# Twenty weight blocks narrowed behind group 0's last tile, and row tile 0's first products of mixture 1 with the weights stationary

## The chip, the cores and the metric

The kernel runs on one core of a Trainium2 chip. The metric is the time of one execution on the device, in microseconds; lower is better. The engines named here are TensorE (PE; PEld is its loading of stationary operands), VectorE (DVE), ScalarE (ACT), GpSimd (POOL) and SyncE (SP), which issues most transfers.

## The reference

Three stages follow one another. Attention over 2 batches of 8 heads, 576 positions and 64 channels keeps the 32 largest scores of each row. Its output, as 1152 tokens of 512 channels, goes through a dense layer pair with SiLU, and the result through eight experts, all of which see every token and are summed with weights from a Sinkhorn normalisation:

```python
scores = scale * np.matmul(q, k.transpose(0, 1, 3, 2))
kth = np.partition(scores, -top_k, axis=-1)[..., -top_k:-top_k + 1]
scores = np.where(scores >= kth, scores, -1000000000.0)
attn = np.exp(scores - np.max(scores, axis=-1, keepdims=True))
attn = attn / (np.sum(attn, axis=-1, keepdims=True) + 1e-09)
x = attn @ v                                   # 1152 x 512
h = x @ w_in                                   # 512 -> 2048
x1 = (h * (1.0 / (1.0 + np.exp(-h)))) @ w_out  # 2048 -> 512
for e in range(E):                             # 8 experts, 512 -> 1024 -> 512
    out += P[:, e:e + 1] * (np.maximum(x1 @ w1[e], 0.0) @ w2[e])
```

The weights w_in and w_out come as 8-byte values; the rest is 4-byte.

## The kernel before

The 1152 tokens are nine row tiles of 128, in five groups: tile 0 alone is group 0, tiles 1 and 2 are group 1, and so on in pairs. For each group, attention goes over four pairs of heads. One score tile (`score_tile`) is 128 rows of one head: TensorE makes the scores (L310), ScalarE copies them (L313), VectorE finds the 32 largest by four MAX8 (L322) with three MATCH_REPLACE between them (L328), ScalarE takes the exponential (L326), VectorE masks and sums (L331) and takes the reciprocal (L334), ScalarE normalises (L335), TensorE transposes in five pieces (L338, L340), ScalarE copies these out (L351, L352), and TensorE multiplies by v (`pav`, L348). For tile 0 the result is x0; for later groups it is split into a high and a low part, xH and xL. The tiles of q are turned by TensorE in a PSUM pool with the tag "pp" and come out as qq and qL.

Mixture 1 (w_in, SiLU, w_out) and the experts follow. For tile 0 mixture 1 is a function of its own, `first_row`, since its weights arrive then. They are 32 blocks of 128 x 512 values, 0.5 MB each; 0 to 15 are w_in (block 4c + F is rows c and columns F), 16 to 31 are w_out. Each is loaded into one of four raw buffers (RAWB, L500) and narrowed to 4 bytes by `narrow`: ScalarE takes the high words (L467), GpSimd (L473), or for each third block ScalarE (L471), the low words into one of CVN buffers cv_n, and VectorE puts the two together (L476). For blocks from LATE on, this last step is issued only behind `held`, the last reciprocal of group 0; the tiles of group 1 wait for the same instruction to be issued. A narrowed copy of each block is written to HBM (L507, `kept_in` and `kept_out`), from which mixture 1 of the later groups reads; all 32 writes are issued behind the last load.

In `first_row` the hides (L518) have x0 as the stationary operand and 512 weight columns moving; F = 0, 1, 2 gather in three PSUM banks, and F = 3 in the bank that F = 0 leaves. A silu is a tanh by ScalarE (L525) and a product by VectorE (L526, gr_m). Its result has tokens on the partitions, so TensorE transposes it (L531) and ScalarE copies it out (L535) before the second products (L540). `x1_tile` then copies x1 (L665), transposes it (L668) and splits it into x1H and x1L, the input of the experts.

Behind that, the kernel fills TensorE's time with expert work on the tiles that are done (FILL): experts 0 to 5 on tile 0, then mixture 1 of group 1, experts 6 and 7 on tile 0, mixture 1 of group 2, and so on. Expert weights come through SP's queue into `raw` (L608) and are split by ScalarE (L135) and GpSimd (L136) into `wa`. The three PSUM banks pass from `first_row` to the experts and the mixtures in this order.

What runs when is decided as the program is built: a scheduler orders each engine's instructions by priorities (`tc.cur_priority`; `conv_at` for narrowings, `keep_at` for the writes), by data and buffers, and by `tc.issue_after`, which keeps an instruction behind another in that ordering. Each engine then runs its own list in order.

## Time and profile before

| | us |
|---|---|
| median of 3 runs | 1257.95 |
| the runs, lowest to highest | 1255.61 to 1258.76 |
| the profiled execution | 1257.62 |
| its span | 1255.8 |
| TensorE busy | 1191.3 (95%) |
| VectorE busy | 811.9 (65%) |
| ScalarE busy | 595.1 (47%) |
| GpSimd busy | 562.9 (45%) |

The page adds up the busy time of each engine over the span. The stretches and timelines further down give the same for parts of it, from the start of the span. A record of the timeline may stand for several instructions of one kind (x4); then its time is from the first one's start to the last one's end. Records of neighbouring instructions overlap, since an instruction starts before the one ahead of it has written its last value. A bracket at the end of a record is idle time ahead of it and what ended that.

### The profile page before, as it was taken

Reading aid. Unit: us, or ns where it says so; the run is one execution under the profiler, and the core shown is the slowest. Engines: PE = TensorE matmul, PEld = TensorE weight load, DVE = VectorE, ACT = ScalarE, POOL = GpSimd, SP = SyncE. Lnnn points to the kernel's source line nnn. Section 1 sums busy time; section 2 is a strip of 40 time slices with the busy share of each in tenths; the row PEclk is TensorE's granted clock in tenths of the full one; section 3 lists DMA queues with packets and bytes.
Section 4 is the critical chain, followed back from the end, with each engine's and each line's share of the span. In section 5 each row is a group of like instructions: output and inputs, shape, how many; then the busy total and the mean of one; then the engine's idle time right before and its main releaser. Section 6 shows DMA issues by size and latency. Waiting matters only on the chain.

```text
span 1255.8 us, 17731 instructions
## 1 busy us (share of the span) xinstructions
PE 1191.3 (95%) x6030; PEld 942.5 (75%) x6030; DVE 811.9 (65%) x1567; ACT 595.1 (47%) x1173; POOL 562.9 (45%) x633
## 2 busy tenths in 40 slices
PE   5868999999999899999998999999999999999998
PEld 3544666688767778889686888888888888888886
DVE  7999999999999999113556434545434445344443
ACT  6855878887866676323313242223322323323221
POOL 6731766678712462320735444344443443353310
PEclk9889999999999999999998999999999999999999
DMA  8994776998776789999724121131121211211002
GB/s 268 296 361 146 231 244 204 323 355 306 240 262 218 241 289 319 325 350 371 264 84 141 53 66 45 41 84 34 52 66 34 75 43 34 68 51 46 23 1 67
DMA packets 131722, 210.90 MB, mean 168 GB/s; under 512 B 23472, under 2 KB 69552, under 8 KB 131632
## 3 DMA queue, kind: packets, MB, share of 16 engines
q1 hardware_dynamic: 131632, 209.77, 50.0%
q8 instruction: 48, 0.79, 0.3%
q14 instruction: 42, 0.34, 0.1%
HBM read 170.15 MB, written 39.58 MB: 167 GB/s over the span
## 4 chain that ended last, share of the span: by engine, by line
PE 75%; DVE 19%; ACT 2%; issue 1%; DMA 1%; POOL 1%; SPq 0%; DVEq 0%; ACTq 0%; POOLq 0%
PE h L145 8%; PE h L146 8%; PE h L144 8%; DVE m L322 6%; DVE w L328 5%; PE bank L144 4%; PE bank L146 4%; PE bank L145 4%; PE yA L146 4%; PE yA L145 4%; PE yA L144 4%; PE yB L144 4%; PE yB L145 4%; PE yB L146 4%; PE bank L582 4%; DVE s L331 2%
## 5 line engine op out<-in xcount | busy, mean ns | idle before, releaser
L136 POOL TENSOR_TENSOR wp<-rw,wp 128x512 fp32r<-128x512 f32 (+1 forms) x56 | 86.2, 1559 | 207.3 <-ACT wp L135 207.3
L322 DVE MAX8 m<-w 128x8 f32<-128x576 f32 x192 | 141.3, 752 | 0.8
L136 POOL TENSOR_TENSOR wa<-raw,wa 128x512 fp32r<-128x512 f32 x88 | 114.8, 1318 | 39.3 <-ACT wa L135 26.9
L136 POOL TENSOR_TENSOR w<-rw,w 128x512 fp32r<-128x512 f32 x56 | 73.0, 1306 | 98.6 <-ACT w L135 98.6
L328 DVE MATCH_REPLACE8 w<-m,w 128x576 f32<-128x576 f32 x128 | 95.2, 746 | 0.0
L144 PE MATMUL yB<-w,gH_0b 128*128 128x512 f32 x208 | 80.9, 389 | 0.0
L145 PE MATMUL yB<-w,gH_0b 128*128 128x512 f32 x208 | 80.9, 389 | 0.0
L951 DVE SCALAR_TENSOR_TENSOR gL_0b<-gB,gH_0b 128x512 fp32r<-128x512 f32 (+1 forms) x56 | 45.2, 808 | 55.1 <-ACT gH_0b L950 54.3
L146 PE MATMUL yB<-w,gL_0b 128*128 128x512 f32 x208 | 80.1, 389 | 0.0
L950 ACT ACTIVATE gH_0b<-gB 128x512 fp32r<-128x512 f32 (+1 forms) x56 | 33.6, 600 | 76.5 <-PE yB L145 43.5
L146 PE MATMUL h<-x1H,wp 128*128 128x512 f32 x168 | 66.9, 398 | 0.0
L144 PE MATMUL h<-x1H,wp 128*128 128x512 f32 x168 | 66.9, 398 | 0.0
L145 PE MATMUL h<-x1L,wp 128*128 128x512 f32 x168 | 66.7, 397 | 0.0
L136 POOL TENSOR_TENSOR gL_m<-g_m,gH_m 128x256 fp32r<-128x256 f32 x48 | 37.6, 783 | 59.7 <-ACT gH_m L135 59.5
L964 DVE TENSOR_TENSOR gB<-u,h 128x512 f32<-128x512 f32 x56 | 38.5, 687 | 37.4 <-PE h L146 37.3
L144 PE MATMUL bank<-xH,wa 128*128 128x256 f32 x192 | 57.1, 297 | 5.9 <-DVE g_m L433 5.7
L135 ACT ACTIVATE w<-rw 128x512 fp32r<-128x512 f32 x56 | 34.7, 627 | 57.4 <-PE yB L146 48.3
L331 DVE SCALAR_TENSOR_TENSOR s<-s,m,e 128x576 f32<-128x576 f32 x64 | 61.7, 963 | 0.3
L326 ACT ACTIVATE e<-s,sm 128x576 f32<-128x576 f32 x64 | 49.9, 781 | 21.8 <-DVE s L331 15.4
L582 PE MATMUL bank<-wb,gT_e 128*128 128x512 f32 x128 | 58.4, 595 | 0.4 <-ACT gT_e L601 0.4
L335 ACT ACTIVATE s<-s,sm 128x576 f32<-128x576 f32 x64 | 50.1, 784 | 16.6 <-DVE sm L334 16.2
L135 ACT ACTIVATE wa<-raw 128x512 fp32r<-128x512 f32 x88 | 54.7, 645 | 1.6 <-DMA raw<-kept_in 0.9
(366 smaller groups left out, 3631.2 us busy)
## 6 DMA issues: line engine op xcount, KB each, us to landing
wa<-sk SPq DMA_DIRECT2D x64, 512.0 KB, 5.4
wb<-sk SPq DMA_DIRECT2D x64, 512.0 KB, 5.1
rw<-in_moe_w_dram SPq DMA_DIRECT2D x112, 256.0 KB, 2.8
raw<-in_moe_w_dram SPq DMA_DIRECT2D x80, 256.0 KB, 3.6
wb<-in_moe_w_dram SPq DMA_DIRECT2D x32, 512.0 KB, 4.6
sk<-wa SPq DMA_DIRECT2D x24, 512.0 KB, 4.0
sk<-wb SPq DMA_DIRECT2D x24, 512.0 KB, 4.5
wfr<-in_moe_w_in_dram SPq DMA_DIRECT2D x16, 512.0 KB, 5.6
```

The source lines that it names most:

```text
L135: nc.scalar.activation(dH, src, AF.Copy)
L136: eng.tensor_sub(dL, src, dH.bitcast(F32))
L144: nc.tensor.matmul(ps, wH, xH, start=first, stop=False, skip_group_check=more)
L145: nc.tensor.matmul(ps, wH, xL, start=False, stop=False, skip_group_check=more)
L146: nc.tensor.matmul(ps, wL, xH, start=False, stop=last, skip_group_check=more)
L322: nc.vector.max(mr, src)
L326: nc.scalar.activation(e, s, AF.Exp, scale=SCALE, bias=sm[:, 0:1])
L328: nc.vector.match_replace(out=w, in_to_replace=mr, in_values=src, imm_value=-3e38)
L331: nc.vector.scalar_tensor_tensor(s, s, m8[:, TOPK - 1 : TOPK], e, op0=ALU.is_ge, op1=ALU.mult, accum_out=sm[:, 1:2])
L335: nc.scalar.activation(s, s, AF.Copy, scale=sm[:, 3:4])
L582: nc.tensor.matmul(y, gT[:, c * P : (c + 1) * P], b[c], start=F == 0 and c == 0, stop=F == nF - 1 and c == NDC - 1)
L951: nc.vector.scalar_tensor_tensor(gL, src, 0.0, gH.bitcast(F32), op0=ALU.max, op1=ALU.subtract)
```

## The change

In `narrow`, LATE falls from 26 to 12, so VectorE's step of 20 blocks, not 6, is issued behind group 0's last reciprocal. CVN grows from 4 to 5, and four more buffers for low words, for blocks 12 to 15, are cut out of the tiles (`cv_xH`, `cv_xL`) that group 1's x uses later. The writes of the first 12 narrowed blocks are issued behind load 24, the other 20 behind the last load.

In `first_row` a weight block of 128 x 128 is now the stationary operand and the 128 rows of x0 move: 64 products in place of 16, and the result has the hidden channels on the partitions. The transposes and their copies (`turned`) are gone. F = 3 has a PSUM bank of its own, taken from the pool "pp" in which q is turned. The silu is written over its own tanh (`g_m0`), and the second products gather in bank 1. `held` becomes the silu of F = 2 once `first_row` is written, so group 1's tiles are issued behind that. `opened`, the copy x1H of tile 0, holds back the normalisations of group 1's first head pair and some of its exponentials. The hides of c = 2, apart from F = 0, come behind the last transposes of group 0.

```diff
-CVN = 4
-LATE = 26
+CVN = 5
+LATE = 12
...
     def evac_split(dH, dL, ps):
-        nc.scalar.activation(dH, ps, AF.Copy)
+        ins = nc.scalar.activation(dH, ps, AF.Copy)
         nc.vector.tensor_sub(dL, ps, dH.bitcast(F32))
+        return ins
...
-                nc.scalar.activation(e, s, AF.Exp, scale=SCALE, bias=sm[:, 0:1])
+                with tc.issue_after(behind.ins) if behind and late else nullcontext():
+                    nc.scalar.activation(e, s, AF.Exp, scale=SCALE, bias=sm[:, 0:1])
...
-        nc.scalar.activation(s, s, AF.Copy, scale=sm[:, 3:4])
+        with tc.issue_after(behind.ins) if behind else nullcontext():
+            nc.scalar.activation(s, s, AF.Copy, scale=sm[:, 3:4])
...
-        nc.tensor.transpose(pt2, s[:, S - P : S], ident)
+        heads.append(nc.tensor.transpose(pt2, s[:, S - P : S], ident))
...
+                                     opened if (g, p) == (1, 0) else None, i == 1)
...
+    spare = []
...
-        n = cvp.tile([P, W], I32, name=f"cv_n_{i}", tag="cvn", bufs=CVN)
+        n = spare.pop(0) if i >= LATE and spare else cvp.tile([P, W], I32, name=f"cv_n_{i}", tag="cvn", bufs=CVN)
...
+        for i in "HL":
+            t = xps[0].tile([P, NDC, 256], F32R, name=f"cv_x{i}", tag=f"x{i}").bitcast(I32).rearrange("p c t -> p (c t)")
+            spare.extend([t[:, :W], t[:, W:]])
...
-        with tc.issue_after(loaded.ins):
-            for i, (d, x) in enumerate(writes):
-                tc.cur_priority = keep_at(i)
+        for i, (d, x) in enumerate(writes):
+            tc.cur_priority = keep_at(i)
+            with tc.issue_after(loads[LATE + CVN + 4 + RAWB - 1 if i < LATE else -1].ins):
                 nc.sync.dma_start(d, x)
         return got
     def first_row(xF, got, pool):
         nF = DFF // W
-        y, gT_ps = banks[0], banks[1]
-        ph = [banks[2], banks[1], banks[0]] + [banks[2]] * (nF - 3)
-        gs, gTs = {}, {}
+        y = banks[1]
+        ph = [banks[2], banks[1], banks[0], ps_p.tile([P, W], F32, name="ph_m0", tag="pp")]
+        gs = {}
         def hide(F, c):
-            nc.tensor.matmul(ph[F], xF[:, c, :], got[0, F, c], start=c == 0, stop=c == NDC - 1)
+            for f in range(NDC):
+                at = slice(f * P, (f + 1) * P)
+                nc.tensor.matmul(ph[F][:, at], got[0, F, c][:, at], xF[:, c, :], start=c == 0 and f == 0,
+                                 stop=c == NDC - 1, skip_group_check=True)
         def silu(F):
             kept = tc.cur_priority
             tc.cur_priority = uid() * 100
-            gs[F] = x1p.tile([P, W], F32, name=f"gr_m0_{F}", tag="x1")
-            t = pool.tile([P, W], F32, name=f"tr_m0_{F}", tag="t", bufs=1)
+            home, tag = ((x1p, "x1"), (pool, "t"))[F // 2]
+            t = gs[F] = home.tile([P, W], F32, name=f"g_m0_{F}", tag=tag)
             nc.scalar.activation(t, ph[F], AF.Tanh, scale=0.5)
-            nc.vector.scalar_tensor_tensor(gs[F], t, 1.0, ph[F], op0=ALU.add, op1=ALU.mult)
+            ins = nc.vector.scalar_tensor_tensor(t, t, 1.0, ph[F], op0=ALU.add, op1=ALU.mult)
             tc.cur_priority = kept
-
-        def turned(F):
+            return ins
+        for c in range(NDC):
+            for F in range(nF - 1):
+                with tc.issue_after(heads[-1].ins) if c == NDC - 2 and F else nullcontext():
+                    hide(F, c)
+        silus = [silu(F) for F in range(nF - 1)]
+        for c in range(NDC):
+            hide(nF - 1, c)
+        silu(nF - 1)
+        for F in range(nF):
             for c in range(NDC):
-                nc.tensor.transpose(gT_ps[:, c * P : (c + 1) * P], gs[F][:, c * P : (c + 1) * P], ident)
-            kept = tc.cur_priority
-            tc.cur_priority = uid() * 100
-            gTs[F] = pool.tile([P, W], F32, name=f"gT_m0_{F}", tag="gT")
-            nc.scalar.activation(gTs[F], gT_ps, AF.Copy)
-            tc.cur_priority = kept
-
-        def second(F):
-            for c in range(NDC):
-                nc.tensor.matmul(y, gTs[F][:, c * P : (c + 1) * P], got[1, F, c], start=F == 0 and c == 0,
+                nc.tensor.matmul(y, gs[F][:, c * P : (c + 1) * P], got[1, F, c], start=F == 0 and c == 0,
                                  stop=F == nF - 1 and c == NDC - 1)
-
-        for c in range(NDC):
-            for F in range(3):
-                hide(F, c)
-        silu(0)
-        silu(1)
-        turned(0)
-        silu(2)
-        for F in range(3, nF):
-            for c in range(NDC):
-                hide(F, c)
-            turned(1)
-            silu(F)
-        for F in range(nF):
-            second(F)
-            if F + 2 < nF:
-                turned(F + 2)
+        return silus[-1]
...
-            first_row(x0, blocks, hp0)
+            held = first_row(x0, blocks, hp0)
...
-            x1_tile(0, banks[0])
+            opened = x1_tile(0, banks[1])
```

How this moves instructions shows on VectorE at the end of group 0's attention. A name such as w_0_0_3_1_0 is group, batch, head pair, head and tile. Before, the last reciprocals are followed by the four narrowings that were held back, and group 1's first MAX:

```order
L322 MAX m8_0_0_3_1_0_585<-w_0_0_3_1_0_584 128x8
L333 TENSOR_SCALAR sm_0_0_3_0_0_553<-sm_0_0_3_0_0_553 128x1
L331 SCALAR_TENSOR_TENSOR s_0_0_3_1_0_582,sm_0_0_3_1_0_586<-s_0_0_3_1_0_582,m8_0_0_3_1_0_585,e_0_0_3_1_0_587 128x576
L334 RECIPROCAL sm_0_0_3_0_0_553<-sm_0_0_3_0_0_553 128x1
L333 TENSOR_SCALAR sm_0_0_3_1_0_586<-sm_0_0_3_1_0_586 128x1
L334 RECIPROCAL sm_0_0_3_1_0_586<-sm_0_0_3_1_0_586 128x1
L476 SCALAR_TENSOR_TENSOR wf_26_630<-wf_26_630,cv_n_26_816 128x512
L476 SCALAR_TENSOR_TENSOR wf_27_629<-wf_27_629,cv_n_27_822 128x512
L476 SCALAR_TENSOR_TENSOR wf_28_628<-wf_28_628,cv_n_28_828 128x512
L476 SCALAR_TENSOR_TENSOR wf_29_627<-wf_29_627,cv_n_29_834 128x512
L322 MAX m8_1_0_0_0_0_1612<-s_1_0_0_0_0_1609 128x8
```

In the changed kernel the same place reads:

```order
L333 SCALAR_TENSOR_TENSOR s_0_0_3_1_0_582,sm_0_0_3_1_0_586<-s_0_0_3_1_0_582,m8_0_0_3_1_0_585,e_0_0_3_1_0_587 128x576
L336 RECIPROCAL sm_0_0_3_0_0_553<-sm_0_0_3_0_0_553 128x1
L335 TENSOR_SCALAR sm_0_0_3_1_0_586<-sm_0_0_3_1_0_586 128x1
L336 RECIPROCAL sm_0_0_3_1_0_586<-sm_0_0_3_1_0_586 128x1
L482 SCALAR_TENSOR_TENSOR wf_12_655<-wf_12_655,cv_xH_625 128x512
L482 SCALAR_TENSOR_TENSOR wf_13_656<-wf_13_656,cv_xH_625 128x512
L482 SCALAR_TENSOR_TENSOR wf_14_657<-wf_14_657,cv_xL_626 128x512
L482 SCALAR_TENSOR_TENSOR wf_15_658<-wf_15_658,cv_xL_626 128x512
L482 SCALAR_TENSOR_TENSOR wf_16_642<-wf_16_642,cv_n_16_754 128x512
L482 SCALAR_TENSOR_TENSOR wf_17_641<-wf_17_641,cv_n_17_760 128x512
L482 SCALAR_TENSOR_TENSOR wf_18_640<-wf_18_640,cv_n_18_766 128x512
L482 SCALAR_TENSOR_TENSOR wf_19_639<-wf_19_639,cv_n_19_772 128x512
```

Behind the last reciprocal stand twelve narrowings in a row (the list shows the first eight), before the first silu. Of the 14 that the change holds back, wf_12 to wf_25, none is left ahead of it; before, these stood among the MAX and MATCH_REPLACE of head pairs 1 to 3.

On TensorE, the end of the hides and the start of the second products. Before (bank0 to bank2 are the three PSUM banks, gr_m0_F the silu of block F, gT_m0_F its transpose):

```order
L518 MATMUL bank2_130<-wf_12_653,x0_86 128x512
L518 MATMUL bank1_129<-wf_13_654,x0_86 128x512
L518 MATMUL bank0_128<-wf_14_655,x0_86 128x512
L518 MATMUL bank2_130<-wf_3_644,x0_86 128x512
L518 MATMUL bank2_130<-wf_7_648,x0_86 128x512
L518 MATMUL bank2_130<-wf_11_652,x0_86 128x512
L518 MATMUL bank2_130<-wf_15_656,x0_86 128x512
L531 MATMUL bank1_129<-ident_58,gr_m0_0_893 128x128 x4
L531 MATMUL bank1_129<-ident_58,gr_m0_1_897 128x128 x4
L540 MATMUL bank0_128<-wf_16_640,gT_m0_0_905 128x512
```

In the changed kernel:

```order
L529 MATMUL bank2_130<-x0_86,wf_12_655 128x128 x4
L529 MATMUL bank1_129<-x0_86,wf_13_656 128x128 x4
L529 MATMUL bank0_128<-x0_86,wf_14_657 128x128 x4
L529 MATMUL ph_m0_879<-x0_86,wf_15_658 128x128 x4
L552 MATMUL bank1_129<-wf_16_642,g_m0_0_928 128x512
L552 MATMUL bank1_129<-wf_17_641,g_m0_0_928 128x512
```

The hides of the last channel block c = 3 now stand together, four pieces for each F, and the second products come right behind them. Before, those of F = 3, for all four c, stood behind the others, and transposes of the silus behind these. Further on in the changed kernel, one score tile, one turning of q and one tile's transposes stand between x1's transposes and expert 0's first product; before, the transposes of four tiles of group 1 and more score tiles went ahead of it.

On SyncE, what stands around load 24. Before, the last loads and the first writes:

```order
L500 DMA wfr_29_831<-in_moe_w_out_dram 128x512
L500 DMA wfr_30_837<-in_moe_w_out_dram 128x512
L500 DMA wfr_31_843<-in_moe_w_out_dram 128x512
L507 DMA kept_in_75<-wf_0_641 128x512
L507 DMA kept_in_75<-wf_1_642 128x512
```

In the changed kernel:

```order
L509 DMA wfr_22_787<-in_moe_w_out_dram 128x512
L509 DMA wfr_23_793<-in_moe_w_out_dram 128x512
L509 DMA wfr_24_799<-in_moe_w_out_dram 128x512
L516 DMA kept_in_75<-wf_0_643 128x512
L516 DMA kept_in_75<-wf_1_644 128x512
```

The twelve writes kept_in of blocks 0 to 11 stand between load 24 and load 25; the other 20 come behind load 31, then three loads of q, then expert 0's first weights.

## Rows read from the trace of the kernel before

**Rows 1.** The page, its first line and its part 1, TensorE

```profile
span 1255.8 us, 17731 instructions
...
PE 1191.3 (95%) x6030; PEld 942.5 (75%) x6030; DVE 811.9 (65%) x1567; ACT 595.1 (47%) x1173; POOL 562.9 (45%) x633
```

**Rows 2.** Stretch: us, busy time and records of each engine, PEclk, DMA share, GB/s

```profile
50.00:60.00 10.00, 8.54 (x42) 6.13 (x41) 10.00 (x22) 8.54 (x17) 6.20 (x6) 0.52 0.76 273
...
80.00:90.00 10.00, 8.35 (x48) 4.76 (x46) 10.00 (x20) 4.34 (x10) 3.30 (x8) 1.00 1.05 403
90.00:100.00 10.00, 6.02 (x19) 3.03 (x20) 10.00 (x23) 5.12 (x9) 0.42 (x2) 1.00 0.92 327
...
110.00:122.30 12.30, 9.29 (x45) 5.75 (x43) 12.27 (x26) 9.45 (x21) 1.91 (x4) 1.00 0.00 1
...
sum 129.90, PE 91.01 PEld 58.74 DVE 121.21 ACT 89.30 POOL 66.28; mean PE 6.50 PEld 4.20 DVE 8.66 ACT 6.38 POOL 4.73
...
sum 1125.90, PE 1100.25 PEld 883.78 DVE 690.69 ACT 505.76 POOL 496.59; mean PE 157.18 PEld 126.25 DVE 98.67 ACT 72.25 POOL 70.94
```

**Rows 3.** Timeline of VectorE: start us, us, line, operation, tiles, count

```profile
77.56 0.16 DVE L334 RECIPROCAL sm<-sm 128x1 f32<-128x1 f32 x1
77.64 1.27 DVE L476 SCALAR_TENSOR_TENSOR wf<-wf,cv_n 128x512 int32<-128x512 int32 x2
```

**Rows 4.** Timeline of TensorE around row tile 0

```profile
87.10 2.74 PE L518 MATMUL bank<-wf,x 128*128 128x512 f32 x6
91.22 3.70 PE L518 MATMUL bank<-wf,x 128*128 128x512 f32 x8 [1.38 <-DVE gr_m L526]
94.75 0.60 PE L531 MATMUL bank<-ident,gr_m 128*128 128x128 f32 x4
...
98.78 2.41 PE L540 MATMUL bank<-wf,gT_m 128*128 128x512 f32 x5 [2.08 <-DVE gr_m L526]
...
122.73 2.38 PE L348 MATMUL pav<-aT,vn 128*64 128x256 f32 x20
...
129.48 0.40 PE L146 MATMUL bank<-wa,x1L 128*128 128x512 f32 x1
```

**Rows 5.** Timeline of ScalarE, its last row of GpSimd

```profile
117.90 0.57 ACT L665 ACTIVATE x<-bank 128x512 f32<-128x512 f32 x1
...
120.02 0.66 ACT L135 ACTIVATE wa<-raw 128x512 fp32r<-128x512 f32 x1
...
125.03 2.55 POOL L136 TENSOR_TENSOR wa<-raw,wa 128x512 fp32r<-128x512 f32 x2
```

**Rows 6.** Timeline of SyncE's queue: issues of transfers

```profile
66.74 2.51 SPq L500 DMA_DIRECT2D wfr<-in_moe_w_out_dram  x4
69.30 12.65 SPq L507 DMA_DIRECT2D kept_in<-wf  x16
...
93.67 2.06 SPq L608 DMA_DIRECT2D raw<-in_moe_w_dram  x4
```

**Rows 7.** By line and form, 0 to 165 us: busy, mean ns | idle before, releaser

```profile
L322 DVE MAX8 m<-w 128x8 f32<-128x576 f32 x63 | 45.9, 748 | 0.1
...
L328 DVE MATCH_REPLACE8 w<-m,w 128x576 f32<-128x576 f32 x42 | 31.1, 742 | 0.0
...
L518 PEld LDWEIGHTS bank<-wf,x 128*128 128x128 f32 x32 | 6.2, 206 | 8.5 <-issue 6.1 <-DVE gr_m L526 2.2 <-ACT x L395 0.2
...
L526 DVE SCALAR_TENSOR_TENSOR gr_m<-tr_m,bank 128x512 f32<-128x512 f32 x4 | 2.7, 676 | 0.0
```

**Rows 8.** Timeline of VectorE, then TensorE, at group 1's end and mixture 1's start

```profile
210.46 0.42 DVE L140 TENSOR_TENSOR xL<-pav,xH 128x256 fp32r<-128x256 f32 x1
...
240.61 0.39 PE L144 MATMUL bank<-xH,wa 128*128 128x256 f32 x1
240.83 0.28 PE L145 MATMUL bank<-xL,wa 128*128 128x256 f32 x1
240.95 0.27 PE L146 MATMUL bank<-xH,wa 128*128 128x256 f32 x1
```

More of the change, by code (lines that the diff above doesn't have):

```diff
@@ L301, in turn_q, with score_tile @@
         return qq, qL, tuple(t[i].rearrange("p (a b) -> p a b", b=P) for t in (qq_half, qL_half))
-    def score_tile(nm, qq, qL, kk, heads, cols, soon):
+    def score_tile(nm, qq, qL, kk, js, cols, soon, behind=None, late=False):
         ps = ps_s.tile([P, 2, 512], F32, name=f"ps_{nm}", tag="s")
-        for j in heads:
+        for j in js:
             for part, a in enumerate((qq, qL)):
@@ L310, in score_tile @@
                     nc.tensor.matmul(ps[:, hh, 0:SH], a[:, j, cols], kk[:, j, hh * SH : (hh + 1) * SH],
-                                     start=j == heads[0] and part == 0, stop=j == heads[-1] and part == 1)
+                                     start=j == js[0] and part == 0, stop=j == js[-1] and part == 1)
         s = sp.tile([P, S], F32, name=f"s_{nm}", tag="s", bufs=SB)
@@ L354, in topk_attention_moe_sinkhorn_kernel @@
     kv = {}
-    copied, normal = [], []
-    held = None
+    copied, normal, heads = [], [], []
+    held = opened = None
     def load(unit):
@@ L481, in first_blocks @@
         nb = 2 * DFF // P
-        got, writes = {}, []
+        got, writes, loads = {}, [], []
+        for i in "HL":
+            t = xps[0].tile([P, NDC, 256], F32R, name=f"cv_x{i}", tag=f"x{i}").bitcast(I32).rearrange("p c t -> p (c t)")
+            spare.extend([t[:, :W], t[:, W:]])
         order = [(0, F, c) for c in range(NDC) for F in range(DFF // W)] + \
@@ L494, in first_blocks @@
             if w_in.dtype == F32:
-                loaded = nc.sync.dma_start(x, (w_in, w_out)[part][r, cols])
+                loads.append(nc.sync.dma_start(x, (w_in, w_out)[part][r, cols]))
             else:
@@ L499, in first_blocks @@
                     tc.cur_priority = int(9.4 * GAP)
-                loaded = nc.sync.dma_start(raw, (w_in, w_out)[part][r, cols])
+                loads.append(nc.sync.dma_start(raw, (w_in, w_out)[part][r, cols]))
                 tc.cur_priority = conv_at(i)
@@ L670, in x1_tile @@
         xH, xL = xH[:, :, cols], xL[:, :, cols]
-        evac_split(xH, xL, pt)
+        return evac_split(xH, xL, pt)
     def logits(tts, pl):
```

2 lines of the change are left out of this document (1 added, 1 removed).

## The prediction

> **What bounds the kernel now.** I read the page first, then the busy time by stretch, then the timelines of the engines around the first row tile. TensorE is busy for 1191.3 of 1255.8 us [rows 1], so a change pays by what it takes from TensorE's work or from its idle time. The stretches say where that idle time lies [rows 2]: up to 129.9 us TensorE works 91.0 us and stands for 38.9; in the 1125.9 us behind, it stands for 25.7 in all. So the start is where something can be had, and what counts is the moment from which TensorE runs without gaps. In the trace this is the first product of expert 0 on row tile 0, whose first hidden block ends at 129.9 [rows 4].
>
> Followed back, that moment hangs on one chain. VectorE is the engine that is never free (10.00 of 10 us from 50 to 60 and from 80 to 100) [rows 2]. On it the last reciprocal of group 0 comes at 77.6, and a narrowing starts right behind it [rows 3]. Then ScalarE normalises, TensorE transposes and multiplies, x0 is done, the last hides of the first three blocks start at 87.10, the silus, the hides of the fourth block (91.22), transposes (94.75) and second products (from 98.78) follow one another through three PSUM banks [rows 4], ScalarE copies x1 at 117.90, TensorE transposes it, and ScalarE cuts expert 0's first weight at 120.02 [rows 4, 5]. DMA is not the bound at the end of this chain: it moves 1 GB/s from 110 to 122 [rows 2], since SP had issued the first weights of expert 0 at 93.67 [rows 6].
>
> **The change part by part.** The sum is made against the profiled execution (1257.6 us with 1.8 outside its span); the median of the runs, 1257.95, is 0.3 above it.
>
> Narrowing behind the last tile. By the order, 14 narrowings and one qL leave the stretch of VectorE's queue ahead of group 0's last reciprocal. Two narrowings take 1.27 [rows 3], so 0.60 to 0.64 each: 15 x 0.60 = 9.0 us, and the reciprocal comes at 77.6 - 9.0 = 68.6. It is bounded on the other side by loads and ScalarE, which serves narrowings of its own ahead of the last exponentials: up to 72. VectorE was full there [rows 2], so what leaves it is gained in whole.
>
> From the reciprocal (call it R) to x0: two normalisations, eight transposes and the product. In the trace x0 is copied at about R + 9, with three 512-column hides and two POOL narrowings standing between; in the new order two hides are left there, which gives R + 5.8.
>
> Hides with the weights stationary. 16 products of 512 columns (32 records, 16.1 us busy) become 64 of 128 (128 records). What one costs with a weight load of 128 columns for each, no row of this form shows. The nearest are transposes, four in 0.60 [rows 4], 0.15 each at most, and mixture 1's products, whose records start 0.12 apart with a fresh 128-column weight each [rows 8]. At 0.12 all 128 records take 15.4 us, within 1 us of what they take now. On the path stand the last 32: 3.8 us, of which the first block needs a quarter. If the loads were not hidden, one would cost the load's 0.21 [rows 7] and the 0.12: 10.6, or 6.8 us more; a gain is excluded, since columns times passes are the same. I take 0.12, as both rows show the load hidden. At a granted clock of 0.52, as from 50 to 60 [rows 2], about the lower of the two levels (1.2 of 2.4 GHz), 3.8 would be 7.4.
>
> On this the Trainium skill speaks against the change: "TensorE: Matmul & The Clock Gate", section "The mechanism", says that a weight load overlaps with running matmuls only when it goes to other row groups, which full 128-row weights never do; in the section "Step-by-step: what each phase is for" it allows the overlap also into the background weight buffer. By the first, the hides would run at load plus product, the 6.8 us of the bound above, and the total would be some 1252; the trace agrees with the second, for mixture 1's full-row weights come 0.12 apart [rows 8].
>
> No turning. The 16 transposes (four in 0.60) and four ScalarE copies go, and so do their places between silus and second products. All four blocks have a PSUM bank each, so that the fourth no longer waits for the first silu (at 91.22, after 1.38 us of idle time) [rows 4]. 16 x 0.12 = 2 us less work for TensorE.
>
> What stands in their place. The second products need weights 16 to 31, whose narrowings are now behind R, one after another on VectorE: rows 110 to 121 of its order take 12 x 0.6 = 7.2, then the silus (0.68 each [rows 7]) come as ScalarE and the loads let them: about R + 8.2, 11, 13.4 and 17.3. Four narrowed blocks lie in spare buffers and five in the common ones, so a raw buffer comes free only as VectorE goes on, and loads 25 to 31 are issued one by one, the last at about R + 13.8 = 82.4 (66.74 to 69.3 before [rows 6]). Its halves are narrowed at R + 23, the last second product is at R + 24.3, x1 at R + 25, its transposes behind a q product at R + 27, x1H at R + 28 = 96.6. So the chain by itself has x1 at 93.6, 24 us sooner than the trace (117.90 [rows 5]).
>
> Expert 0's weights are what comes late then. On SP 12 writes of kept weights go ahead of load 25, and 20 stand behind load 31. 16 of them take 12.65 us there [rows 6]; at 0.68 to 0.79 each, 20 end at 96 to 98. Three q loads follow, and the first weights are issued at about 98, against 93.67; six blocks of 0.26 MB at 403 GB/s [rows 2] land in 3.9, so at 102. On ScalarE the first cut of a weight stands behind a normalisation that waits for group 1's first reciprocal. On VectorE that is 46 instructions behind R: 20 x 0.62 + 4 x 0.68 + 11 x 0.75 + 8 x 0.74 + 2.4 = 31.7 [rows 3, 7], with short waits for silus and loads 33, so 101.8. Then come two exponentials, and the first cut at 104. POOL's half of a cut takes 1.28 (two in 2.55) [rows 5] and the first block needs four, with products following each: its hidden block ends at about 110.8. That is **19 us earlier** than 129.9. Bounds: 104 if weights were there at once, 116 if R is at 72 and the queue slips by 2.
>
> What was done meanwhile. Before 129.9 the trace has also done attention work of group 1 that the new order puts behind expert 0's first block: one product with v (2.38 [rows 4]), three or four tiles' transposes (0.6 for four) and three score tiles with q products, for which I put 2.5: 7 us of TensorE. This must still be done, so the net lead is 19 - 7 = **12 us**. The other way round: 91 - 7 - 2 = 82 us of work ends at 110.8, idle 29 in place of 38.9, plus the 2 us of transposes, again 12.
>
> Is the lead kept? Behind 129.9 TensorE has 2% idle [rows 2]; it is the bound. Attention must stay ahead of it: group 1's last value is there at 210.46, mixture 1 uses it from 240.61 [rows 8], 30 us of slack, of which the lead takes 12 and VectorE's new waits of 2 or 3 us the rest of little. So 1257.6 - 12 = **1245.5**.
>
> **The rivals.** (a) *The lead goes.* Loads 25 to 31 wait for a raw buffer, this for POOL and ScalarE, these for a narrowed buffer, this for VectorE, and VectorE's next silu for TensorE: a ring in which each turn costs its latency. For it speaks that 20 blocks turn in it; against it that nine buffers hold the first. At 1 us more for each of seven turns, and the writes behind them, 8 to 11 us go: 1254 to 1257.
>
> (b) *Slower: group 1 starves VectorE.* The fourth block's bank comes from the pool in which q is turned, and it is held until the fourth silu at R + 17, so the q of group 1's next head pairs can't be made; normalisations and exponentials of its first pair stand behind x1H. VectorE, which never idles in the trace, then idles, and every microsecond of this moves attention's end. It decides once the idle time eats the slack left, 30 - 12 = 18 us; at 24 it gives 1257.6 + 6 = 1264. Against it: the order puts the second pair's q right in the second products, and narrowings fill VectorE.
>
> (c) *The whole chain counts.* The writes go faster and ScalarE does not wait; then the block ends at 104, and by the same account 1257.6 - 19 = 1238; with deferred work hidden in gaps, 1235.
>
> (d) *The hides are no faster.* Loads aren't hidden: 6.8 us of the 12 go, 1252; at half clock also 1249 to 1254.
>
> **How the numbers follow.** The forecast, 1241 to 1251 with its bounds, has 0.52; (a) 0.17; (b) 0.11; (c) 0.13; (d) 0.07. A measurement here tells 0.3%, 3.8 us, from no change: below 1254.2 is faster, which takes the forecast, (c) and (d): 0.72; same is (a), 0.17; slower is (b), 0.11. The range leaves out (b) and the far end of (c): 1234 to 1257.
>
> **What would show it.** In the new profile the last L336 reciprocal of group 0 should be at 67 to 72, the hides' records some 0.12 apart, no transposes between silu and second product, the first product of expert 0 at 104 to 107 and its first hidden block at 108 to 114, and TensorE's idle time up to there near 29 us and behind it still near 25. If the hides' records are 0.2 or more apart, (d) is right; if VectorE shows several microseconds of idle time after 100, (b); if the last load comes after 88, (a). The forecast fails if TensorE's idle time behind the first block grows by what was won ahead of it.

## The result

The changed kernel takes 1241.66 us (median of 4 runs, 1240.83 to 1241.85) against 1257.06 for the kernel before: a ratio of 0.9875, interval 0.9864 to 0.9887, so 15.4 us less. A second measurement on another chip gave 1240.57 and a ratio of 0.9876 (0.9856 to 0.9897). The forecast was 1245.5, 12 us less, with 1234 to 1257 as its range.

The page of the changed kernel answers to [rows 1]: the span is 15.7 us shorter, TensorE is busy 5.3 us less and idle 10.4 us less (54.1 against 64.5).

```profile
span 1240.1 us, 17869 instructions
...
PE 1186.0 (96%) x6110; PEld 950.1 (77%) x6110; DVE 810.9 (65%) x1567; ACT 591.4 (48%) x1169; POOL 566.9 (46%) x633
```

Where that idle time lies shows in the busy time by stretch: up to the first relu of expert 0 (at 113.85, the copy that ends its first hidden block), to 283, to 480 and to the end. Columns are as in [rows 2].

```profile
0.00:113.85 113.85, 81.22 (x425) 60.30 (x425) 102.95 (x225) 75.63 (x145) 65.58 (x74) 0.91 0.89 294
113.85:283.00 169.15, 168.34 (x959) 122.33 (x960) 162.70 (x360) 139.48 (x300) 121.93 (x151) 0.99 0.84 276
283.00:480.00 197.00, 189.12 (x1239) 154.07 (x1238) 196.85 (x446) 144.09 (x303) 95.13 (x141) 1.00 0.81 273
480.00:1240.10 760.10, 747.36 (x3492) 613.40 (x3491) 348.44 (x539) 232.16 (x423) 284.29 (x269) 0.99 0.31 101
```

The same cuts in the kernel before (its relu at 129.94) leave TensorE idle for 38.9, 1.5, 10.4 and 13.7 us; here it is 32.6, 0.8, 7.9 and 12.7. So 6.3 us of idle time went ahead of the relu and 4.2 behind it.

The steps of the chain follow, engine by engine. On VectorE the last reciprocal of group 0, the narrowings behind it, the first and the last silu, and group 1's first reciprocal (compare [rows 3]):

```profile
67.02 0.16 DVE L336 RECIPROCAL sm<-sm 128x1 f32<-128x1 f32 x1
67.09 1.27 DVE L482 SCALAR_TENSOR_TENSOR wf<-wf,cv_xH 128x512 int32<-128x512 int32 x2
68.29 1.29 DVE L482 SCALAR_TENSOR_TENSOR wf<-wf,cv_xL 128x512 int32<-128x512 int32 x2
69.49 3.09 DVE L482 SCALAR_TENSOR_TENSOR wf<-wf,cv_n 128x512 int32<-128x512 int32 x5
...
77.68 0.69 DVE L538 SCALAR_TENSOR_TENSOR g_m<-g_m,bank 128x512 f32<-128x512 f32 x1 [1.16 <-ACT g_m L537]
...
84.69 0.67 DVE L538 SCALAR_TENSOR_TENSOR g_m<-g_m,ph_m 128x512 f32<-128x512 f32 x1
...
101.28 0.14 DVE L336 RECIPROCAL sm<-sm 128x1 f32<-128x1 f32 x1
```

The reciprocal came at 67.0, 10.5 us before the 77.56 of the kernel before, and the first nine held narrowings then run in a row, 0.62 each.

On TensorE (compare [rows 4]) a v product of head pair 2, hides of c = 2, the v product of the last pair, the hides of c = 3 in two records, the start of the second products, and the end of expert 0's first hidden block:

```profile
65.81 2.15 PE L351 MATMUL pav<-aT,vn 128*64 128x128 f32 x20
...
72.26 1.95 PE L529 MATMUL bank<-x,wf 128*128 128x128 f32 x16
74.14 1.31 PE L351 MATMUL pav<-aT,vn 128*64 128x128 f32 x20
75.86 2.94 PE L529 MATMUL bank<-x,wf 128*128 128x128 f32 x24 [0.40 <-ACT x L399]
78.64 1.06 PE L529 MATMUL ph_m<-x,wf 128*128 128x128 f32 x8
79.85 9.71 PE L552 MATMUL bank<-wf,g_m 128*128 128x512 f32 x22 [0.15 <-DVE g_m L538]
...
110.68 0.40 PE L147 MATMUL bank<-wa,x1L 128*128 128x512 f32 x1
```

On ScalarE (compare [rows 5]) a copy of x0's third part, the two last normalisations of group 0, x0's last part, x1, its high part x1H, the wait for group 1's first reciprocal, the first cut of an expert weight, and the relu:

```profile
68.03 0.28 ACT L399 ACTIVATE x<-pav 128x128 f32<-128x128 f32 x1 [1.41 <-PE pav L351]
68.21 1.43 ACT L338 ACTIVATE s<-s,sm 128x576 f32<-128x576 f32 x2
...
75.53 0.28 ACT L399 ACTIVATE x<-pav 128x128 f32<-128x128 f32 x1 [1.85 <-PE pav L351]
...
94.58 0.60 ACT L662 ACTIVATE x<-bank 128x512 f32<-128x512 f32 x1 [3.95 <-PE bank L552]
...
96.09 0.62 ACT L139 ACTIVATE x1H<-bank 128x512 fp32r<-128x512 f32 x1
101.46 0.78 ACT L338 ACTIVATE s<-s,sm 128x576 f32<-128x576 f32 x1 [4.75 <-DVE sm L336]
102.14 1.43 ACT L328 ACTIVATE e<-s,sm 128x576 f32<-128x576 f32 x2
103.61 0.63 ACT L135 ACTIVATE wa<-raw 128x512 fp32r<-128x512 f32 x1
...
113.85 0.58 ACT L589 ACTIVATE gr_e<-bank 128x512 f32<-128x512 f32 x1
```

And SyncE's queue (compare [rows 6]):

```profile
56.83 9.45 SPq L516 DMA_DIRECT2D kept_in<-wf  x12
73.70 8.09 SPq L509 DMA_DIRECT2D wfr<-in_moe_w_out_dram  x7
81.88 2.88 SPq L516 DMA_DIRECT2D kept_in<-wf  x4
84.86 13.14 SPq L516 DMA_DIRECT2D kept_out<-wf  x16
...
100.14 1.49 SPq L604 DMA_DIRECT2D raw<-in_moe_w_dram  x3
```

x1 is there at 94.6 and x1H at 96.7, but the first weight is cut at 103.6: of the two things that expert 0 needs, the input is there 7 us ahead of the weights. Two waits end together ahead of that cut. ScalarE waits for group 1's first reciprocal and then takes two exponentials, until 103.6; and the first weights, issued at 100.14, land 3.5 us later, also at 103.6. Two later cuts wait for their transfers again, 0.67 and 1.36 us.

### The profile page after: what moved, and what is told of

Same layout as the page of the kernel before. It is cut to its first block, busy times and chain, and to the rows that moved or that the text cites. A ratio compares the mean times of both kernels' runs of the same rounds, so it can differ in the third digit from the quotient of the medians.

```text
span 1240.1 us, 17869 instructions
## 1 busy us (share of the span) xinstructions
PE 1186.0 (96%) x6110; PEld 950.1 (77%) x6110; DVE 810.9 (65%) x1567; ACT 591.4 (48%) x1169; POOL 566.9 (46%) x633
## 4 chain that ended last, share of the span: by engine, by line
PE 79%; DVE 15%; ACT 2%; DMA 2%; issue 1%; SPq 1%; POOL 0%; DVEq 0%; ACTq 0%; POOLq 0%
PE h L146 9%; PE h L147 9%; PE h L145 9%; DVE m L323 5%; PE bank L145 5%; PE bank L147 4%; PE bank L146 4%; PE yA L147 4%; PE yA L146 4%; PE yA L145 4%; PE yB L145 4%; PE yB L146 4%; PE yB L147 4%; PE bank L578 4%; DVE w L330 4%; PE pav L351 2%
## 5 line engine op out<-in xcount | busy, mean ns | idle before, releaser
L136 DVE TENSOR_TENSOR wp<-sp,wp 128x1024 fp32r<-128x1024 f32 x28 | 44.7, 1597 | 16.5 <-ACT wp L135 16.5
```

Of the source, the lines that this page charges most:

```text
L136: eng.tensor_sub(dL, src, dH.bitcast(F32))
```

## The experiments

Each is the changed kernel with one edit. The relu stands for the moment at which TensorE gets its steady work (113.85 in the changed kernel, 129.94 before). Each ratio is against the kernel before, measured beside it (medians of 1256.1 to 1257.6).

**Fewer narrowings held back.** LATE goes back from 12 to 26, with the split of the writes kept.

```diff
-LATE = 12
+LATE = 26
...
-            with tc.issue_after(loads[LATE + CVN + 4 + RAWB - 1 if i < LATE else -1].ins):
+            with tc.issue_after(loads[24 if i < 12 else -1].ins):
```

> The changed kernel, but only 6 of the 32 narrowings are held behind group 0's last reciprocal, as before; hides, banks and the split of the writes stay as in the changed kernel. My account: the reciprocal goes back from 67 to about 77, but what follows it gets shorter, since no row of narrowings stands ahead of the silus and the writes end sooner; x1 is copied near 101 (94.6 in the changed kernel, 117.9 before), expert 0's first hidden block ends at 113 to 116 in place of 111, and the time is 1244 to 1247. Rival, the held-back narrowings are the gain: all 10 us of the reciprocal come back, x1 at 104 or later, 1250 to 1252. Rival, they gain nothing since expert 0's weights set the start: 1240 to 1243.

Measured: 1249.37, ratio 0.994 (0.9926 to 0.9955). So what is left of the change gains 6.8 us without the 14 narrowings. On VectorE, the last reciprocal of group 0 and the first silu:

```profile
77.80 0.17 DVE L336 RECIPROCAL sm<-sm 128x1 f32<-128x1 f32 x1
...
87.86 0.69 DVE L538 SCALAR_TENSOR_TENSOR g_m<-g_m,bank 128x512 f32<-128x512 f32 x1 [3.31 <-ACT g_m L537]
```

and on ScalarE x1 and x1H:

```profile
103.65 0.60 ACT L662 ACTIVATE x<-bank 128x512 f32<-128x512 f32 x1 [11.52 <-PE bank L552]
104.99 0.60 ACT L139 ACTIVATE x1H<-bank 128x512 fp32r<-128x512 f32 x1 [0.26 <-PE bank L665]
```

The reciprocal is at 77.8 as expected, x1 at 103.7 rather than 101, the relu at 118.8 rather than 113 to 116, and the time lies between the two accounts. The x1 chain was mis-sized by 2.7 us; the first silu is 10 us behind the reciprocal here as in the changed kernel, though only 6 narrowings are left.

**The first row tile's products as before, with the narrowings held back.** This is the other half of the change alone: `first_row` is that of the kernel before.

```diff
-CVN = 5
+CVN = 4
...
-        y = banks[1]
-        ph = [banks[2], banks[1], banks[0], ps_p.tile([P, W], F32, name="ph_m0", tag="pp")]
+        y, gT_ps = banks[0], banks[1]
+        ph = [banks[2], banks[1], banks[0]] + [banks[2]] * (nF - 3)
...
-            for f in range(NDC):
+            nc.tensor.matmul(ph[F], xF[:, c, :], got[0, F, c], start=c == 0, stop=c == NDC - 1)
...
```

> The changed kernel with the first row tile's mixture 1 of the kernel before: x0 stationary, block F = 3 in the bank that F = 0 leaves, 16 transposes and 4 copies; one buffer for low words fewer, for room. Narrowings are held back as in the change. My account: the reciprocal stays near 67, x1 comes at 104 to 108 (the chain from reciprocal to x1 is 40 us in the kernel before and 27.5 in the changed one), which is now behind expert 0's weights, so the first hidden block ends at 117 to 122, and the time is 1248 to 1253. Rival, the weights of expert 0 set the start and the chain is hidden: only the transposes' 2 us come back, 1243 to 1244.

Measured: 1246.09, ratio 0.9916 (0.9899 to 0.9932), 10.1 us below the kernel before. On ScalarE, x1 and x1H:

```profile
101.46 0.60 ACT L677 ACTIVATE x<-bank 128x512 f32<-128x512 f32 x1 [6.21 <-PE bank L550]
102.80 0.60 ACT L139 ACTIVATE x1H<-bank 128x512 fp32r<-128x512 f32 x1 [0.75 <-PE bank L680]
```

x1 came at 101.5, sooner than I had put it (104 to 108), and the relu at 116.0, so the time fell between the two accounts again. The halves alone gain 6.8 and 10.1 us, both together 15.4: nearly the sum. They aren't wholly separate, though: both runs keep the split of the writes and the holds on group 1, and no run has these alone. Without the turned form x1 is 6.9 us later, the relu only 2.2. In the profile the loss of 4.6 us stands in TensorE's busy time (1191.0 against 1186.0), not in its idle time (53.7 against 54.1).

**No bank of the pool for q.** Block F = 3 gathers behind F = 0 in bank 2.

```diff
-        ph = [banks[2], banks[1], banks[0], ps_p.tile([P, W], F32, name="ph_m0", tag="pp")]
+        ph = [banks[2], banks[1], banks[0], banks[2]]
```

> The changed kernel, but block F = 3 gathers in bank 2 behind F = 0, so no bank of the pool in which q is turned is held by it. My account: F = 3's hides wait for the first silu, the last silu comes 2 to 4 us later, x1 1 to 3 us later, which expert 0's weights mostly hide: 1241 to 1244. Rival, holding that bank starves VectorE of group 1's work: q is turned sooner, VectorE's first reciprocal of group 1 comes 2 us or more before 101, and the time falls to 1237 to 1240.

Measured: 1243.14 (1239.75 to 1244.8), ratio 0.989 (0.9872 to 0.9907): no difference from the change that these intervals show. The last silu moved by 3.6 us (88.26), x1H by 1.8, and the relu came at 112.5, not later: x1 has slack against the weights. Holding the bank doesn't starve VectorE, whose first reciprocal of group 1 comes at 100.8 in place of 101.3.

**All writes behind the last load.** The only edit is when the 32 narrowed blocks may be written.

```diff
-            with tc.issue_after(loads[LATE + CVN + 4 + RAWB - 1 if i < LATE else -1].ins):
+            with tc.issue_after(loads[-1].ins):
```

> The changed kernel, but all 32 writes of narrowed blocks are issued behind the last load, as before. My account: SP stands idle for raw buffers before load 25 anyway, so the loads come no sooner; 32 writes in place of 20 stand between the last load and expert 0's first weights, these are issued at about 108 in place of 100, the first hidden block ends near 119, and the time is 1247 to 1250. Rival, ScalarE's wait for group 1's first reciprocal (101) sets the start and the weights have time in hand: 1241 to 1243.

Measured: 1260.48, ratio 1.0032 (1.0019 to 1.0045). This one line takes the whole gain and more. SyncE's queue:

```profile
49.80 33.07 SPq L509 DMA_DIRECT2D wfr<-in_moe_w_out_dram  x13
82.93 11.83 SPq L516 DMA_DIRECT2D kept_in<-wf  x16
94.85 10.90 SPq L516 DMA_DIRECT2D kept_out<-wf  x16
...
107.88 1.49 SPq L604 DMA_DIRECT2D raw<-in_moe_w_dram  x3
```

and ScalarE, x1H and the first cut:

```profile
97.99 0.62 ACT L139 ACTIVATE x1H<-bank 128x512 fp32r<-128x512 f32 x1
...
111.30 0.63 ACT L135 ACTIVATE wa<-raw 128x512 fp32r<-128x512 f32 x1 [7.93 <-DMA raw<-in_moe_w_dram]
```

The loads end 1 us later and x1H is there at 98.6, 1.9 later. But 32 writes stand ahead of expert 0's first weights, these are issued at 107.9 in place of 100.1, and ScalarE waits 7.93 us for their landing; the relu is at 123.9. This run shows that the place of the weights behind the writes can set the start, since they are what ScalarE waits for here. It doesn't show that they alone set it in the changed kernel, where ScalarE's wait ends at the same time; in the second profile of that kernel (the last run below) the first weights landed at 102.7 and ScalarE came to them only at 103.6. The loss is more than twice what I had put: 10 us up to the relu, and behind it TensorE's idle time grew from 21.4 to 28.7 us; its granted clock was 0.50 from 110 to 120, after 9.13 us of idle time.

**Some writes between the last loads.**

```diff
-            with tc.issue_after(loads[LATE + CVN + 4 + RAWB - 1 if i < LATE else -1].ins):
+            with tc.issue_after(loads[24 if i < LATE else min(31, i + 13)].ins):
```

> The changed kernel, but the writes of blocks 12 to 18 are issued one behind each of the loads 25 to 31 (by the order, seven of the twenty stand between those loads) in place of all behind the last. My account, by which expert 0's weights set the start since their transfers wait for the writes: transfers are idle for half of 70 to 80, so the writes end 3 to 4 us sooner, the first weights are issued at 96 to 97 in place of 100.1; the first cut on ScalarE still waits for group 1's first reciprocal at 101, but those behind it don't wait for their transfers any more, and the first hidden block's relu comes at 110 to 112 in place of 113.85: 1238.5 to 1240.5. Rival, the writes delay loads 25 to 31 by as much as they gain: x1 later than 96 and 1241 to 1244.

Measured: 1247.97, ratio 0.9929 (0.9916 to 0.9943). The edit didn't do what it was for: the last load was issued at 85.1 in place of 81.8, the first weights at 98.3, the next three at 101.6. The relu moved by 0.8 (114.66), so neither account is told apart by it. Yet the time is 6 us above the changed kernel. TensorE's sum:

```profile
sum 1246.70, PE 1193.29 PEld 955.02 DVE 804.99 ACT 591.79 POOL 567.09; mean PE 298.32 PEld 238.75 DVE 201.25 ACT 147.95 POOL 141.77
```

It is idle for 53.4 us, as in the changed kernel (54.1), but busy for 7.3 us more with the same instructions; 3.6 of these stand in the records of the products with v. Of the 3.6, 1.1 lie between 50 and 60, where the granted clock was 0.62 in place of 0.80; why the others took longer is open.

**Part of the writes out of the way.** The right halves of blocks 16 to 31 of `kept_out` are filled ahead of load 25 from other weights, and only the left halves written behind the last load.

```diff
-                nc.sync.dma_start(d, x)
+                nc.sync.dma_start(d if i < 16 else d[:, : W // 2], x if i < 16 else x[:, : W // 2])
+            if i >= 16:
+                tc.cur_priority = keep_at(0)
+                with tc.issue_after(loads[24].ins):
+                    nc.sync.dma_start(d[:, W // 2 :], w2[0][(i - 16) % 8 * P : ((i - 16) % 8 + 1) * P, : W // 2])
```

> The changed kernel, but only the left half of blocks 16 to 31 is written to HBM behind the last load; the right halves are filled ahead of load 25, where the transfers stand idle, from other weights (so mixture 1 of the later groups multiplies by weights that are partly not its own; the work is the same). This takes 2 MB from the queue between the last load and expert 0's first weights. My account, by which the weights wait for those writes and set the start: first weights issued at 94 to 96 in place of 100.1, relu of the first hidden block at 109 to 112 in place of 113.85 (x1H at 96 to 98 and ScalarE's wait for the reciprocal of 101 hold the rest): 1236 to 1240. Rival, ScalarE's wait sets the start: relu within 1 us of 113.85, 1241 to 1243. Since changes at the start moved the idle time of TensorE between 283 and 480 by up to 6 us in earlier runs, the relu decides, not the total.

Measured: 1247.06, ratio 0.9921 (0.9908 to 0.9934). Inconclusive for the same reason: SyncE took 10.6 us for the fills, some of the first writes slid behind load 25, the issue of the last four loads ended at 85.8, and the first weights went out at 99.2. The relu came at 114.5, within the rival's 1 us, but with the weights issued only 0.9 sooner this doesn't speak for it.

**Expert 0's cuts ahead of group 1's first normalisations.** `opened` is the cut of the fourth weight block in place of x1H.

```diff
-            opened = x1_tile(0, banks[1])
+            x1_tile(0, banks[1])
...
+        if g == 0:
+            opened = cuts[3]
```

> The changed kernel, but the normalisations of group 1's first head pair are held behind the cut of expert 0's fourth weight block in place of x1H, so that no wait for VectorE stands ahead of the cuts on ScalarE. My account: the weights land at 102 to 107, so the first cuts come 1 to 2 us sooner and the relu at 112 to 113.5 in place of 113.85; group 1's attention moves back by some us, which its slack takes: 1239.5 to 1242. Rival, ScalarE's wait for the reciprocal (4.75 us in the changed kernel) is what sets the start: relu at 109 or sooner, 1236 to 1238.5.

Measured: 1249.65, ratio 0.9943 (0.993 to 0.9956). ScalarE no longer stands behind the reciprocal; it waits 5.11 us for the weights instead (first cut 105.6), which here are issued at 102.4, as the loads ended 2.8 us later in the new order. The relu is at 117.7. Both accounts named a sooner relu and both were wrong. Since the weights themselves are 2.2 us later here, the wait for them doesn't tell which of the two waits counts in the changed kernel.

**A number between.** 14 narrowings held back, 12 writes behind load 24.

```diff
-LATE = 12
+LATE = 18
...
-            with tc.issue_after(loads[LATE + CVN + 4 + RAWB - 1 if i < LATE else -1].ins):
+            with tc.issue_after(loads[24 if i < 12 else -1].ins):
```

> The changed kernel with 14 narrowings held back in place of 20 (6 gave 1249); 12 writes behind load 24, 20 behind the last load, as in the changed kernel. My account has two chains that meet at expert 0's first product: with 20 held back the weights come last (x1H 96.7, first cut 103.6), with 6 x1 comes last (weights issued at 90.8, x1H 105). In between both come sooner than the later one: reciprocal at 70 to 72, x1H at 98 to 100, weights issued at 94 to 96, relu at 109 to 112, 1237.5 to 1240.5. Rival, the time simply follows the number held back: 1244 to 1246.

Measured: 1245.6 (1243.61 to 1248.08), ratio 0.9914 (0.9898 to 0.993). The time is the rival's. The last reciprocal and the first silu on VectorE:

```profile
72.18 0.17 DVE L336 RECIPROCAL sm<-sm 128x1 f32<-128x1 f32 x1
...
86.90 0.69 DVE L538 SCALAR_TENSOR_TENSOR g_m<-g_m,bank 128x512 f32<-128x512 f32 x1 [0.70 <-ACT g_m L537]
```

The reciprocal is where I expected it and the weights are issued at 94.0, but the first silu is 14.7 us behind the reciprocal, not 10. In VectorE's order all 14 narrowings, wf_18 to wf_31, stand ahead of the first silu here, and VectorE is idle for 7 of the 15 us from 75 to 90, 4.6 of them waiting for GpSimd's low words; in the changed kernel only wf_12 to wf_23 do, and the others stand among the silus and behind them. So x1 came at 103.9 and the relu at 117.6. x1 is no sooner than with 6 held back (103.7), so the rival's account, that the time follows the number held back, isn't shown by its number.

**Group 1 held behind the reciprocal, as before.**

```diff
-            held = first_row(x0, blocks, hp0)
+            first_row(x0, blocks, hp0)
```

> The changed kernel, but group 1's tiles are held behind group 0's last reciprocal, as before, in place of the silu of F = 2. My account: four MAX8 and some more of group 1 stand on VectorE ahead of the silus, which come 2 to 4 us later, so x1H comes at 98 to 101, still ahead of the weights at 103.6; group 1 gets ahead by the same: 1241 to 1243.5. Rival, x1's chain sets the start: 1244 to 1247.

Measured: 1253.43, ratio 0.9976 (0.9966 to 0.9987). x1 came at 94.9 and the relu at 114.5, within 1 us of the changed kernel, and still 12 of the 15 us are gone. Busy time by stretch, with the cuts used above:

```profile
0.00:114.51 114.51, 78.41 (x427) 58.62 (x428) 104.64 (x229) 77.74 (x150) 68.76 (x76) 0.91 0.90 299
114.51:283.00 168.49, 167.47 (x959) 120.55 (x958) 165.66 (x366) 137.31 (x295) 121.91 (x148) 1.00 0.81 268
283.00:480.00 197.00, 182.96 (x1194) 147.97 (x1193) 196.81 (x447) 142.43 (x303) 94.83 (x140) 1.00 0.77 260
480.00:1251.40 771.40, 757.45 (x3537) 621.76 (x3535) 346.37 (x529) 232.14 (x424) 285.80 (x271) 0.99 0.31 104
```

TensorE is idle for 36.1 us up to the relu (2.8 us less work is done by then), and for 14.0 in place of 7.9 between 283 and 480. Neither account had this: both looked no further than the first block. Group 1's first reciprocal came at 96.5 here, so ScalarE did not stand behind it; it waited 3.46 us for the first weights, issued at 98.0, and cut them at 102.3, 1.3 us sooner than in the changed kernel, and still the relu came no sooner.

**Without the hold of the first normalisations.**

```diff
-                                     opened if (g, p) == (1, 0) else None, i == 1)
+                                     None, i == 1)
```

> The changed kernel without the hold of group 1's first normalisations and exponentials behind x1H. My account: ScalarE's order around x1H stays nearly the same (three rows move), x1H comes at 96 to 98, the relu at 113 to 115; any difference in time comes from later: 1240 to 1246. Rival, the hold is what keeps x1 ahead: x1H at 100 or later and 1247 or more.

Measured: 1246.31, ratio 0.9914 (0.99 to 0.9928). x1H was issued at 102.5, 6 us later than with the hold, as the rival had it, but the relu came at 113.2, as I had it: the 7 us of slack again. The 4 us lie behind, 3.3 us of TensorE's idle time between the relu and 283 in place of 0.8 and 1.7 us more of its busy time.

**Every hide twice.**

```diff
-                nc.tensor.matmul(ph[F][:, at], got[0, F, c][:, at], xF[:, c, :], start=c == 0 and f == 0,
-                                 stop=c == NDC - 1, skip_group_check=True)
+                for n in range(2):
+                    nc.tensor.matmul(ph[F][:, at], got[0, F, c][:, at], xF[:, c, :], start=c == 0 and f == 0 and n == 0,
+                                     stop=c == NDC - 1 and n == 1, skip_group_check=True)
```

> The changed kernel with each of the 64 hides issued twice (the first products of row tile 0 then count double). Prices the hides and shows how much slack x1 has against expert 0's weights. My account: 128 more records at 0.12 are 15 us of TensorE work, most of it in its idle time ahead of x0; on the path the last 32 cost 4 us, x1H comes at 100 to 101, still ahead of the first cut (103.6), so the relu moves by 0 to 2 us; with less idle time left, 1243 to 1249. Rival, weight loads are not hidden when hides stand in a long row: records 0.2 or more apart, x1H at 104 or later, 1252 or more.

Measured: 1253.01, ratio 0.9968 (0.9954 to 0.9981). TensorE's longest row of hides:

```profile
80.68 5.62 PE L530 MATMUL bank<-x,wf 128*128 128x128 f32 x48 [0.96 <-ACT x L399]
```

48 records in 5.62 us are 0.117 each, though each has a weight load of its own, 0.19 us by its record: no sign of loads that aren't hidden. TensorE is busy for 13.9 us more, 0.11 for each of the 128 records added. x1H moved by 7.4 us to 103.5, more than the 4 I had put, the relu by 4.5 us to 118.3; the slack of 7 us took part of it. The time is 4 us above the range that I had given.

**The change once more.**

> The changed kernel unaltered, as a control for the variants, which came out 1 to 12 us above its first measurement with expert 0's first relu within some us of its 113.85. My account: the relu again at 113 to 115, TensorE's idle time between 283 and 480 again near 8 us, 1240 to 1243.5, so that differences of 4 us and more between variants belong to the order of their instructions. Rival, such differences come from one chip or run to the next: 1245 or more.

Measured: 1240.57, ratio 0.9876 (0.9856 to 0.9897). The relu was at 112.6, just below the expected 113, and TensorE idle for 7.8 us between 283 and 480. It was busy for 1182.9 us, 3.1 less than in the first profile (1186.0), so differences of this size in its busy time say nothing. So the 4 to 12 us by which variants lie above it, with relus at 113 to 115, belong to the variants.

## Why the prediction was right, point by point

**What bounds.** Right: TensorE's idle time ahead of its steady work was the place. Up to the end of the first hidden block (111.1) it is 30.4 us, 29 forecast.

**The reciprocal.** 68.6 forecast, 67.0 measured. Holding back freed at least the whole of the narrowings' time on VectorE (9.0 us by the sum, 10.5 measured); where the other 1.5 come from isn't shown.

**From there to x0.** Forecast R + 5.8, measured R + 8.5 (75.5). ScalarE stood 1.41 us for the v product of the pair before, which TensorE ran in 2.15 us (1.31 for the last pair's, also 20 records), and 16 hides of c = 2 took 1.95 ahead of the last v product. This term was mis-sized by 2.7 us, and slack hid it.

**Hides.** Right: 24 records in 2.94, 0.12 each, and doubling them costs 0.11 to 0.12 each. All 128 records together are busy for 17.1 us (15.4 forecast, 16.1 before). Rival (d) is not borne out: a row of 48 records, each with its own load of a full 128 x 128 block, runs at 0.117, where load and product one after the other would take some 0.31 (0.19 and 0.117). The sentence that a weight load overlaps with running matmuls only when it goes to other row groups, from "TensorE: Matmul & The Clock Gate" of the Trainium skill (section "The mechanism"), is not borne out by these rows.

**The narrowed blocks.** The last load was to go out at 82.4 and the record of the last seven ends at 81.8; first silu R + 10.7 (8.2 forecast), last R + 17.7 (17.3), x1 at 94.6 (93.6). The ring of rival (a) costs 2.5 us at the first silu and 0.4 at the last.

**The weights last.** Right in its times: first weights issued at 100.1 (98), group 1's first reciprocal at 101.3 (101.8), first cut 103.6 (104), end of the first hidden block 111.1 (110.8), 18.8 us ahead of the kernel before (19). That x1 is not what counts is shown: without the hold of the first normalisations x1H came 6 us later and the relu 0.7 sooner. That the writes ahead of the weights can set the start is shown by the run with all writes behind the last load. Which of the weights and ScalarE's wait for the reciprocal sets it in the changed kernel is open, since both end at 103.6, and the two runs meant to bring the weights sooner did so by only 1.8 and 0.9 us. The sum had the wait for the reciprocal last, with the weights there at 102; that the two end together was not foreseen.

**From 19 to 12.** Here the sum was off: 15.7 in the profiled spans. It had 2 us less work for TensorE and 10 us less idle time; measured are 5.3 and 10.4 (8.4 and 9.7 in the second profile of the changed kernel). So the 3.4 us beyond the forecast stand in TensorE's busy time, about as much as it differs between two profiles of one kernel. The transposes' records are 2.5 us, 2 forecast. In the records, most of the rest stands in the products with v, 3.0 us less, which ran in part at a lower granted clock before (0.52 from 50 to 60 in [rows 2]; 0.80 in the same stretch now). That this is the cause is an argument, not shown.

**Is the lead kept?** It was, and group 1's slack held as argued. Its last value on VectorE and the first product of mixture 1 that uses it (compare [rows 8]):

```profile
214.14 0.41 DVE L140 TENSOR_TENSOR xL<-pav,xH 128x256 fp32r<-128x256 f32 x1
...
222.49 0.68 PE L145 MATMUL bank<-xH,wa 128*128 128x256 f32 x1
```

That leaves 8 us of the 30; the sum, 12 for the lead and 2 or 3 for new waits, would leave 15. But the argument stopped there, and the runs show more: with the relu within 1.5 us of 113.85, five variants came out at 1243, 1246, 1247, 1248 and 1253. So how much of the lead is kept rests on the order of the work behind it. For the one at 1253, the loss shows as TensorE's idle time from 283 to 480, 14.0 us against 7.9 in the changed kernel (10.4 before), in a stretch where VectorE is busy for 196.8 of 197 us in both. For the other four that idle time is 7.0 to 8.6 us, and their losses lie elsewhere: the one at 1248 has 7.3 us more of busy time. What in an order makes the one or the other wasn't settled, and that the change itself came out at the low end was not forecast: that part is luck.

**The rivals.** (a) and (d) are ruled out by the rows above. (b) did not happen: with the bank given back, VectorE gained 0.5 us. (c) did not happen either: the chain alone would have had the input there 7 us sooner than the first cut, and the weights and ScalarE's wait held it.

**Slips in the working.** With R at 68.6, R + 33 is 101.6, not 101.8. Rival (b) at 24 us of idle time eats 6 of the 12 us won, which by its own slack is 1251.5, not 1264. That VectorE never idles holds for the stretches shown; from 129.94 to 283 it was idle for 8.6 us in the kernel before. And 1234 as the low end of the range does not leave out (c)'s far end, 1235. None of these moves the forecast.

## What to carry to other kernels

When a chain shortens, look at once for what else its end needs: here the weights stood behind 20 writes in one queue, and where those writes stood was worth 19 us, more than the change. Side work of a full engine can be held behind the instruction on the path: here 14 narrowings more held back brought the last reciprocal 10.8 us sooner (77.8 to 67.0) and the time down by 7.7. But look at what then stands behind it: with 8 of the 14 held, x1 came no sooner. And measure a few edits around a change before reading the last microseconds of its time as its own: the order made by a scheduler moved the end by up to 12 us with the start within 1.5 us of where it was.

## What the runs showed of the hardware

Rows of products with 128 moving columns, each record with its own load of a 128 x 128 block of 4-byte values, run at 0.117 to 0.12 us per record, so four of them cost what one 512-column record does (eight in 3.70, 0.46 each [rows 4]).

TensorE's clock fell in the changed kernel where the one before had it whole. Stretches, columns as in [rows 2]:

```profile
90.00:100.00 10.00, 7.77 (x30) 4.27 (x29) 10.00 (x22) 2.72 (x5) 2.11 (x5) 0.91 1.04 398
100.00:105.00 5.00, 2.03 (x6) 1.21 (x6) 5.00 (x12) 3.49 (x6) 1.28 (x3) 0.50 0.81 242
105.00:110.00 5.00, 4.43 (x14) 3.15 (x13) 5.00 (x12) 3.00 (x7) 4.84 (x5) 0.65 0.90 309
```

It works for 7.8 of the 10 us from 90 to 100 and is granted 0.50 from 100 to 105 (2.0 of 5 us busy) and 0.65 from 105 to 110, so that expert 0's first products run partly at the lower of the two levels: 0.63 each for records that take 0.40 further on. With all writes last it was idle for 9.13 us and granted 0.50 from 110 to 120. The kernel before was busy for only 6.0 of the 10 us from 90 to 100 [rows 2] and was granted 1.00 from there to 110, so the busy share of such a stretch alone doesn't tell whether the clock falls.
